# A two-layer decode step on one core: four loads merged into larger ones

## The chip, the cores and the metric

The kernel runs on one core of a Trainium2 chip. The metric is device time in microseconds; the runs of the kernel before agree within 0.1%. Engines are named as the profile names them: PE (matrix multiply), DVE (vector), ACT (activation), POOL (GpSimd), SP (the queue that issues the loads) and 16 DMA engines that carry them.

## The reference

One token (a vector of 512 numbers) goes through two layers with the same weights and the same caches. Each layer is an attention block over a cache of 4096 keys and values in 32 heads of 128, and a dense block with gelu, each behind a layer norm and with a residual. All is float32.

```python
def _A_ref(x, k_cache, v_cache, wq, wo):          # 32 heads, Sk = 4096, Dh = 128
    q = (x @ wq).reshape(B, Sq, H, Dh).transpose(0, 2, 1, 3)
    scores = einsum("bhqd,bhkd->bhqk", q, k_cache) * (Dh ** -0.5)
    p = softmax(scores, axis=-1)
    o = einsum("bhqk,bhkd->bhqd", p, v_cache)
    return o.transpose(0, 2, 1, 3).reshape(B, Sq, H * Dh) @ wo
def _B_ref(x, w1, b1, w2, b2):                    # 512 -> 1376 -> 512
    return einsum("bsf,fd->bsd", gelu(einsum("bsd,df->bsf", x, w1) + b1), w2) + b2
x = x + _A_ref(layernorm(x), k, v, wq, wo)
x = x + _B_ref(layernorm(x), w1, b1, w2, b2)
x = x + _A_ref(layernorm(x), k, v, wq, wo)
x = x + _B_ref(layernorm(x), w1, b1, w2, b2)
```

The keys and values of a layer are 134 MB and don't fit on the core, so almost all of them are read twice.

## The kernel before, in words

The 32 heads are taken in `G = 8` groups of four (`J = 4`). A group's K, and its V, is 8 MB: `C = 8` chunks of 1 MB, each of four quarters (one head each, `U = 512` columns); `NC = 4 * U` is one chunk's width. All large data lie in one tile, `arena`. It holds a ring of three places of 8 MB (`A_AT`, `C_AT`, `B_AT`) for K and V in turn; behind them stand `SHARED`, `SCRATCH`, `TURNED`, `PAIR` (weights of the queries and of the output for one group) and `KEPT_K`.

All loads are issued by SP through one helper (L108), in the order of the program, and SP waits in that order: a load that must wait for its place to come free holds every later one. A load is a DMA of 128 rows.

For a group, `scores` multiplies each chunk of K (8 matmuls in the trace per chunk) into the PSUM tile `pS`, `exponentials` and `weights` make the softmax weights (DVE, ACT, PE in a chain; the last copy is L247), and `values` multiplies each chunk of V into `pO`, again 8 matmuls per chunk. For most groups only two chunks of V go through PE (`partly`) and DVE does the rest. The helper `blocks(src, g, home, pieces)` loads a block in the given pieces and yields its chunks; PE can begin a chunk when its piece has landed. Without `pieces` the block comes as one load. `head` (DVE L286 to L294) turns `pO` into the heads' outputs.

Layer one goes through the groups 0 to 7. Its last group (`final`) loads K as two halves (`HALVES`) and V in the pieces of `LAST` (4, 2, 1 and 1 chunks), and runs all of V on PE. Behind it come `wo`, W1 in four loads and, in `mlp`, W2 in five loads, each issued when PE has read the part of W1 that lay there; `behind_w2` issues the next loads while PE runs through W2. The fourth load of W1 overlaps `SCRATCH` and so waits on SP for DVE L290.

Layer two begins with the groups 7 and 6: V of both, K of group 7 and some of K of group 6 are still on the core. What is missing of K of group 6 is fetched by `begin_k(home, n)`, `n` quarters (of 0.25 MB) at a time. Two such loads of four quarters go to `C_AT`, the place of the K that PE is reading in the scores of group 7, chunk by chunk; each is issued behind the chunk that it overwrites. Then the groups 5 to 0 follow, the last with `HALVES` and `LAST` again, and then `wo`, W1 and W2, here all in places of their own.

`idle` is a matmul by zeros that keeps PE busy between pieces of V; its result is not used.

Of the kernel before, what the change touches and what calls it, by code (L numbers as in the profile page):

```python
# [23 lines left out]
C = 8  # L24
# [5 lines left out]
NC = 4 * U  # L30
# [7 lines left out]
A_AT, B_AT, C_AT = RING  # L38
# [7 lines left out]
HALVES = ((0, 4), (4, 8))  # L46
# [4 lines left out]
FRONT = 192  # L51
CELLS = 239
W1_AT_END = ((0, 2), (2, 3), (3, 4))
LAST = ((0, 4), (4, 6), (6, 7), (7, 8))
W2_AT_CHANGE = ((0, 2), (2, 5), (5, 8), (8, 10), (10, 11))
W2_AT_END = ((0, 4), (4, 8), (8, 10), (10, 11))

# [2 lines left out]
def decode_layers(ctx: ExitStack, tc: tile.TileContext, vectors, k, v, w, w1, w2, out):  # L60
# [42 lines left out]
    def at(first, n):  # L103
        return arena[:, first : first + n]

    def load(first, src):
        t = at(first, src.shape[-1])
        tc.keep_in_program_order(nc.sync.dma_start(t, src))  # L108
        return t
# [4 lines left out]
    def quarters(first):  # L114
        return [at(first + U * j, U) for j in range(4)]

    def part(src, g, a, b):
        return src[g][:, NC * a : NC * b]

    def of_w(row, i, n):  # L120
        return w[row][:, NC * i : NC * (i + n)]
# [33 lines left out]
    def of_32(t, n, i=0):  # L155
        return t[:, : 32 * n].rearrange("p (c q) -> p c q", q=32)[:, :, i]
# [4 lines left out]
    def pairs(t):  # L161
        return t[:, :8].rearrange("p (c i) -> p c i", i=2)
# [61 lines left out]
    def scores(z, c, kt):  # L224
        for j in range(J):
            matmul(pS[32 * j : 32 * j + C, :], z[:, C * j + C - 1 - c : C * j + 2 * C - 1 - c], kt[j],
                   start=(c == 0), stop=(c == C - 1))

    def exponentials(sc, nsc, between=None):
        nc.vector.tensor_reduce(ml[:, 0:1], pS, axis=AX.X, op=ALU.max)  # L230
        m, bias = small("m"), mt
        nc.vector.transpose(mt, ml)
        nc.vector.tensor_reduce(m, mt[:, :C], axis=AX.X, op=ALU.max)
        nc.vector.tensor_scalar(mb[:, :C], m.to_broadcast([P, C]), nsc, None, op0=ALU.mult)  # L234
        nc.vector.transpose(bias, mb)  # L235
        if between:
            between()
        p = at(SCRATCH, U)
        nc.scalar.activation(p, pS, AF.Exp, bias=bias[:, 0:1], scale=sc, accum_out=ml[:, 0:1])  # L239
        return p  # L240
# [39 lines left out]
    def sum_up(t):  # L280
        for j in range(J):
            matmul(pO[32 * j : 32 * j + 4, :], one.to_broadcast([P, 4]), t[j], start=False, stop=True)

    def head(rl, last=False):
        ot = at(SCRATCH, U)
        nc.vector.transpose(ot, pO)  # L286
        o, on = small("o", 4), on_wide
        own = at(SCRATCH, 4 * 129).rearrange("p (b q) -> p b q", q=129)[:, :, :P]
        own = own.rearrange("p b (d q) -> p d b q", q=32)[:, :, :, 0]
        nc.vector.tensor_reduce(o, own, axis=AX.X, op=ALU.add)  # L290
        if last:
            nc.vector.tensor_scalar(on[:, :4], o, rl, None, op0=ALU.mult)  # L292
        else:
            nc.vector.tensor_scalar(in_quarters(on, 4), o.unsqueeze(1).to_broadcast([P, J, 4]), rl, None,  # L294
                                    op0=ALU.mult)
        return on
# [7 lines left out]
    def out_product(on, wt, to, narrow=False):  # L304
        for d in range(4):
            if narrow:
                for j in range(J):
                    matmul(to[32 * j : 32 * j + 1, :P], on[:, d : d + 1], wt[:, d, P * j : P * (j + 1)],
                           start=(d == 0), stop=(d == 3))
            else:  # L310
                matmul(to, on[:, d : d + P], wt[:, d, :], start=(d == 0), stop=(d == 3))
# [47 lines left out]
    def blocks(src, g, home, pieces=((0, C),)):  # L359
        for a, b in pieces:  # L360
            load(home + NC * a, part(src, g, a, b))
            for c in range(a, b):
                yield c, quarters(home + NC * c)
# [29 lines left out]
    def add_up(acc, own):  # L393
        t = small("acc", 4)
        nc.vector.scalar_tensor_tensor(t, own, 1.0, acc, op0=ALU.mult, op1=ALU.add)
        return t


    def group(z, acc, ahead, k_blocks, out_behind=C - 2):
        for c, t in k_blocks:  # L400
            scores(z, c, t)
            if ahead and c == SUM_BEHIND:
                t, rl, wt = ahead
                sum_up(t)
                on = head(rl)
            if ahead and c == out_behind:
                out_product(on, wt, pO)
        p = exponentials(sc, nsc)
        if ahead:
            acc = add_up(acc, of_32(turned(pO, wide=True), 4))  # L410
        return acc, *weights(p)
# [8 lines left out]
    negm, z, sc, nsc = first_queries(xs, s, wq_t, wide=True)  # L420
    acc = pairs(xs)[:, :, 0]
    ahead = None
    for g in range(G):
        final = g == G - 1
        k_home, v_home = RING[2 * g % 3], RING[(2 * g + 1) % 3]
        acc, pt, rl = group(z, acc, ahead, blocks(k, g, k_home, HALVES if final else ((0, C),)))
        ahead = None
        if g == G - 2:
            nc.scalar.copy(at(KEPT_K, 2 * U), at(k_home + NC * C - 2 * U, 2 * U))
        if g < G - 2:  # L430
            partly(pt, blocks(v, g, v_home), v_home)
            pair = load(PAIR, of_w(g % 2, g, 2))
            z = next_queries(xs, negm, by_four(pair[:, NC:]), to=pS)
            ahead = added(v_home), rl, by_four(pair[:, :NC])
            continue
        for c, t in blocks(v, g, v_home, LAST if final else ((0, C),)):
            values(c, pt, t, c)
            if final and c in (5, 7):
                idle(pS)
            if g == G - 2:  # L440
                for j in range(J):
                    i = 4 * c + j - KEPT_V // U
                    if i >= 0:
                        nc.scalar.copy(pK[i], t[j])
        if final:
            wo_t = by_four(load(PAIR, of_w(g % 2, g, 1)))
            for i in range(3):
                load_w1(SHARED, i, i + 1)
            own = head_out(rl, wo_t, last=True, home=ident)
            load_w1(SHARED, 3, 4)  # L450
        else:
            pair = load(PAIR, of_w(g % 2, g, 2))
            acc = add_up(acc, head_out(rl, by_four(pair[:, :NC])))
            wq_t = by_four(pair[:, NC:])
            z = next_queries(xs, negm, wq_t)
# [5 lines left out]
    def begin_k(home, n):  # L461
        a = len(k_t)
        load(home, k[G - 2][:, U * a : U * (a + n)])
        k_t.extend(at(home + U * i, U) for i in range(n))
# [16 lines left out]
    g = G - 2  # L481
    negm, z, sc, nsc = first_queries(xs, s, wq_t)
    make_identity(nc, ident)
    acc = pairs(xs)[:, :, 0]
    wq_t = by_four(at(SHARED, NC))
    begin_k(PAIR + NC, 4)
    for c in range(C):
        scores(z, c, quarters(C_AT + NC * c))
        if c < 2:
            begin_k(C_AT + NC * c, 4)  # L490
        if c == 5:
            begin_k(C_AT + 2 * NC, 12)
            k_t += [at(KEPT_K, U), at(KEPT_K + U, U)]
# [5 lines left out]
    pt, rl = weights(p)  # L499
# [3 lines left out]
    acc = add_up(acc, of_32(turned(pO), 4))  # L503
# [8 lines left out]
    pt, rl = weights(exponentials(sc, nsc))  # L512
    for c in range(C):
        values(c, pt, v_t[4 * c : 4 * c + 4], c)
    acc = add_up(acc, head_out(rl, by_four(pair[:, NC:])))
    z = next_queries(xs, negm, by_four(pair[:, :NC]))

    turned_at[0] = at(TURNED, P)
    homes, ahead = (A_AT, C_AT, B_AT), None
    for n in range(2, G):  # L520
        g, final = G - 1 - n, n == G - 1
        k_home, v_home = homes[(2 * n - 1) % 3], homes[2 * n % 3]
        acc, pt, rl = group(z, acc, ahead, blocks(k, g, k_home, HALVES if final else ((0, C),)),
                            C - 1 if final else C - 2)
        if not final:
            by_pe = BY_PE_AT_BEGIN if n == 2 else BY_PE
            partly(pt, blocks(v, g, v_home, ((0, 6), (6, 8)) if n == 2 else ((0, C),)), v_home, by_pe)
            pair = load(PAIR, of_w(g % 2, g - 1, 2))
            z = next_queries(xs, negm, by_four(pair[:, :NC]), to=pS)
            ahead = added(v_home, by_pe), rl, by_four(pair[:, NC:])  # L530
            continue
        for c, t in blocks(v, g, v_home, LAST):
            values(c, pt, t, c)
            if c in (5, 7):
                idle(pS)
        wo_t = by_four(load(PAIR, of_w(g % 2, g, 1)))
        for a, b in W1_AT_END:
            load_w1(A_AT, a, b)
        for a, b in W2_AT_END:
            load_w2(A_AT + 11 * U, a, b)  # L540
        own = head_out(rl, wo_t, last=True)
# [46 lines left out]
```

## Time and profile before

| | |
|---|---|
| median of 3 runs | 673.24 us (672.96 to 673.5) |
| profiled execution: span | 670.3 us, 2.9 us under the median of the runs |
| mean granted clock of PE | 0.793 |
| PE, DVE, ACT, POOL busy | 384.4, 372.6, 22.8, 4.8 us |
| load queue | 11088 packets, 285.61 MB, 99.1% of 16 engines' span |

The profiled execution has no time of its own other than its span (first to last instruction); what lies around it is the difference to the median. In the rows below, a line of the timeline has the start, the length, the engine, the line of the program, the operation, what it writes and reads, how many instructions were merged, and in brackets the idle time before it and what ended that. A chain's line has start, length, and what the time went to. Times are in us from the start of the span.

### The profile page before, as it was taken

To read this page: it belongs to the slowest core of one execution; us is meant where nothing else is said; L and a number is where in the kernel's file an instruction comes from. 1 tells how busy PE (TensorE), PEld (TensorE's weight loads), DVE (VectorE), ACT (ScalarE), POOL (GpSimd) and SP (SyncE) were. 2 spreads that over 40 slices of the span, in tenths; PEclk is the share of its full clock that TensorE was granted. 3 is DMA by queue.
4 is the path that set the end of the run, shared out by engine and by line. 5 is a ranking of instruction groups with operands and counts; after the bars stand their busy time and mean duration, and the time that the engine had idled before them with its cause. 6 is when DMAs were issued, how large, how long until landed. Compare 5 with 4: busy or idle time off the path is not lost. (4 is left out here: it accounts for less than half of the span.)

```text
span 670.3 us, 5537 instructions
## 1 busy us (share of the span) xinstructions
PE 384.4 (57%) x2342; PEld 109.2 (16%) x2342; DVE 372.6 (56%) x480; ACT 22.8 (3%) x48; POOL 4.8 (1%) x23
## 2 busy tenths in 40 slices
PE   3533842636618546286768878737617456074586
PEld 1101210101102101021214222111102112011122
DVE  2059388395793965932112221392893966938822
ACT  0010000000000000002000110000000000000000
POOL 1000000000000000000000000000000000000000
PEclk9567785877678658778979998977669868687789
DMA  9999999999999999999999999999999999999996
GB/s 376 438 439 438 434 438 438 405 464 435 438 430 408 430 438 439 438 438 421 426 416 402 431 452 423 437 440 431 426 434 416 457 439 438 435 423 407 438 420 286
DMA packets 11256, 285.97 MB, mean 427 GB/s; under 512 B 1504, under 2 KB 1504, under 8 KB 3296
## 3 DMA queue, kind: packets, MB, share of 16 engines
q1 hardware_dynamic: 11088, 285.61, 99.1%
q8 instruction: 18, 0.29, 0.2%
q14 instruction: 6, 0.05, 0.0%
q10 hardware_dynamic: 144, 0.01, 0.0%
HBM read 285.62 MB, written 0.00 MB: 426 GB/s over the span
## 5 line engine op out<-in xcount | busy, mean ns | idle before, releaser
L264 DVE TENSOR_TENSOR arena<-arena 128x2048 f32<-128x2048 f32 (+4 forms) x44 | 260.7, 5924 | 16.6 <-DMA arena<-in_v 15.9
L112 PE MATMUL pS<-arena,front 128*8 128x512 f32 x1036 | 152.0, 713 | 174.9 <-DMA arena<-in_k 164.5
L112 PE MATMUL pO<-arena 128*4 128x512 f32 x504 | 81.7, 800 | 26.1 <-DMA arena<-in_v 24.5
L112 PE MATMUL pO<-arena,cells 128*128 128x512 f32 (+4 forms) x376 | 82.7, 506 | 17.2 <-POOL cells L186 6.7
L112 PEld LDWEIGHTS pS<-arena,front 128*8 128x8 f32 x1036 | 30.6, 102 | 289.1 <-DVE arena L264 141.9
L286 DVE STREAM_TRANSPOSE arena<-pO 128x512 f32<-128x512 f32 x16 | 11.5, 717 | 110.1 <-PE pO L112 110.1
L112 PE MATMUL pS<-arena,cells 128*1 128x128 f32 (+1 forms) x328 | 55.8, 385 | 18.5 <-DMA arena<-in_w 15.8
L170 DVE STREAM_TRANSPOSE arena<-pO 32x128 f32<-32x128 f32 x64 | 20.0, 312 | 59.0 <-PE pO L112 58.4
L112 PEld LDWEIGHTS pO<-arena,cells 128*128 128x128 f32 (+3 forms) x376 | 28.7, 122 | 64.7 <-issue 35.8
L230 DVE TENSOR_REDUCE cells<-pS 128x1 f32<-128x512 f32 x16 | 11.1, 692 | 50.1 <-PE pS L112 49.8
L244 PE MATMUL pO<-front,arena 128*128 128x128 f32 x64 | 12.0, 318 | 46.2 <-ACT arena L239 46.2
L112 PEld LDWEIGHTS pS<-arena,cells 128*1 128x1 f32 (+1 forms) x328 | 23.9, 120 | 61.2 <-issue 52.8
L239 ACT ACTIVATE arena<-pS,cells 128x512 f32<-128x512 f32 x16 | 12.4, 777 | 507.1 <-DVE cells L235 507.1
L112 PEld LDWEIGHTS pO<-arena 128*4 128x4 f32 x504 | 13.5, 99 | 76.2 <-issue 66.3
L244 PEld LDWEIGHTS pO<-front,arena 128*128 128x128 f32 x64 | 7.6, 154 | 60.2 <-ACT arena L239 59.1
L170 DVE STREAM_TRANSPOSE arena<-pS 32x128 f32<-32x128 f32 x44 | 13.7, 312 | 1.6
L249 DVE STREAM_TRANSPOSE cells<-cells 128x32 f32<-128x32 f32 x16 | 3.4, 214 | 15.9 <-ACT arena L239 15.7
L390 DVE MEMSET pS<- 128x512 f32 x11 | 5.3, 485 | 1.2
L174 DVE STREAM_TRANSPOSE arena<-pS 128x128 f32<-128x128 f32 x3 | 1.0, 317 | 8.9 <-PE pS L112 8.9
L199 DVE TENSOR_SCALAR cells<-cells,pS 128x4 f32<-128x4 f32 x4 | 0.9, 234 | 7.9 <-PE pS L112 7.9
L112 PE MATMUL pO<-arena,front 128*128 128x128 f32 (+2 forms) x18 | 5.1, 382 | 0.0
L247 DVE COPY arena<-pO 128x128 f32<-128x128 f32 x16 | 4.2, 261 | 0.7 <-PE pO L244 0.5
(62 smaller groups left out, 72.5 us busy)
## 6 DMA issues: line engine op xcount, KB each, us to landing
arena<-in_w SPq DMA_DIRECT2D x13, 2048.0 KB, 11.2
arena<-in_k SPq DMA_DIRECT2D x4, 4096.0 KB, 24.9
arena<-in_v SPq DMA_DIRECT2D x2, 4096.0 KB, 38.7
arena<-in_w SPq DMA_DIRECT2D x6, 1024.0 KB, 21.1
arena<-in_v SPq DMA_DIRECT2D x3, 2048.0 KB, 42.5
arena<-in_v SPq DMA_DIRECT2D x1, 6144.0 KB, 30.2
arena<-in_w SPq DMA_DIRECT2D x6, 688.0 KB, 25.9
arena<-in_v SPq DMA_DIRECT2D x4, 1024.0 KB, 46.0
```

The lines of the kernel that those rows point to most:

```text
L112: tc.keep_in_program_order(nc.tensor.matmul(*a, **kw))
L170: turn = nc.vector.transpose(t[q], src[q, P * j : P * (j + 1)])
L174: nc.vector.transpose(t, src[:, :P])
L199: nc.vector.tensor_scalar(xc, pairs(xs)[:, :, 0], nm, None, op0=ALU.add)
L230: nc.vector.tensor_reduce(ml[:, 0:1], pS, axis=AX.X, op=ALU.max)
L239: nc.scalar.activation(p, pS, AF.Exp, bias=bias[:, 0:1], scale=sc, accum_out=ml[:, 0:1])
L244: tc.keep_in_program_order(nc.tensor.transpose(pT[:, b].rearrange("p j r -> p (j r)"), p[:, P * b : P * (b + 1)], ident))
L247: nc.vector.tensor_copy(pt, pT[:, :, :, :C].rearrange("p b j c -> p c j b"))
L249: nc.vector.transpose(lt, ml)
L264: tc.keep_in_program_order(nc.vector.tensor_tensor(*a, **kw))
L286: nc.vector.transpose(ot, pO)
L390: nc.vector.memset(pS, 0.0)
```

## The change

Four loads fewer, with the same bytes to the same places:

1. K of the last group of layer one is one load instead of two halves. (Layer two's last K keeps its halves.)
2. V of the last group of layer one is three loads of five, two and one chunks, instead of four loads of four, two, one and one.
3. The same for V of the last group of layer two, by the same constant `LAST`. In both, one `idle` matmul pair moves from behind chunk 5 to behind chunk 6.
4. At the change of layers, two loads of four quarters of group 6's third piece of K become one of eight. It is issued behind chunk 1 of the scores instead of behind chunks 0 and 1.

```diff
-LAST = ((0, 4), (4, 6), (6, 7), (7, 8))
+LAST = ((0, 5), (5, 7), (7, 8))
...
-        acc, pt, rl = group(z, acc, ahead, blocks(k, g, k_home, HALVES if final else ((0, C),)))
+        acc, pt, rl = group(z, acc, ahead, blocks(k, g, k_home))
...
         for c, t in blocks(v, g, v_home, LAST if final else ((0, C),)):
             values(c, pt, t, c)
-            if final and c in (5, 7):
+            if final and c in (6, 7):
                 idle(pS)
...
         scores(z, c, quarters(C_AT + NC * c))
-        if c < 2:
-            begin_k(C_AT + NC * c, 4)
+        if c == 1:
+            begin_k(C_AT, 8)
         if c == 5:
             begin_k(C_AT + 2 * NC, 12)
...
         for c, t in blocks(v, g, v_home, LAST):
             values(c, pt, t, c)
-            if c in (5, 7):
+            if c in (6, 7):
                 idle(pS)
```

## The prediction, on record before the result

> **What bounds the kernel now.** I read the page first (the slices, the queues, the issues), then the chain that ended last, then the stages that the edits touch, as a timeline. The page says what kind of kernel this is:
>
> ```profile
> span 670.3 us, 5537 instructions
> DMA  9999999999999999999999999999999999999996
> GB/s 376 438 439 438 434 438 438 405 464 435 438 430 408 430 438 439 438 438 421 426 416 402 431 452 423 437 440 431 426 434 416 457 439 438 435 423 407 438 420 286
> q1 hardware_dynamic: 11088, 285.61, 99.1%
> HBM read 285.62 MB, written 0.00 MB: 426 GB/s over the span
> ```
>
> The DMA engines are busy in every slice until the last. Slices that carry only large transfers move 438 GB/s; nothing in the span is faster for long. So this is one stream of 285.6 MB, and PE and DVE matter only where they are late in freeing room for it. The chain agrees:
>
> ```profile
> 601.86 45.74 DMA arena<-in_v
> 647.60 0.02 issue
> 647.61 18.66 DMA arena<-in_w
> 666.27 0.04 issue
> 666.32 0.62 PE pS L112 x16
> ```
>
> From the last issues of V to 666.27 the end is the ring emptying itself; only some 4 us of compute stand behind it. An edit can therefore gain in two ways (less overhead inside the stream, a shorter tail) and lose in one (the ring runs dry because an issue came too late). The sum is made against the profiled execution: span 670.3, and the median 673.24 stands 2.9 above it; I take that margin as unchanged.
>
> **The price of a transfer.** The calls to the loading helper, by source, and its quickest landing:
>
> ```profile
> L108 SPq DMA_DIRECT2D arena<-in_w x33: 327/328/432, 0.7 to 651.2; - x33
> L108 SPq DMA_DIRECT2D arena<-in_k x22: 327/382/453, 1.2 to 600.4; - x22
> L108 SPq DMA_DIRECT2D arena<-in_v x21: 327/328/432, 13.1 to 602.3; - x21
> DMA to landing us min/median/max: 4.9/27.9/55.9
> ```
>
> 76 loads and the store of the result make 77 transfers, and 11088 packets / 77 = 144 per transfer, 9 on each of 16 engines. Upper bound of the price: at 438 GB/s the bytes alone need 652 us; the stream runs from about 2 to 666.3, so 12.3 us are overhead of every kind, 0.16 per transfer. Lower bound: nothing. For the value I use the last V of the first layer, where three pieces follow each other and PE waits for the first and for the last of them:
>
> ```profile
> 322.31 3.70 PE L112 MATMUL pO<-arena,cells 128*128 128x512 f32 x8 [1.58 <-DVE cells L395]
> 327.65 7.05 PE L112 MATMUL pS<-arena,front 128*8 128x512 f32 x64 [1.65 <-DVE front L220]
> 331.03 0.18 PEld L112 LDWEIGHTS pS<-arena,front 128*8 128x8 f32 x8 [0.68 <-DMA arena<-in_k]
> 338.22 0.27 DVE L247 COPY arena<-pO 128x128 f32<-128x128 f32 x1
> 340.82 7.25 PE L112 MATMUL pO<-arena 128*4 128x512 f32 x48 [2.66 <-DMA arena<-in_v]
> 348.00 1.12 PE L112 MATMUL pS<-arena,front 128*128 128x512 f32 x2
> 350.46 1.04 PE L112 MATMUL pO<-arena 128*4 128x512 f32 x8 [0.36 <-DMA arena<-in_v]
> 351.57 0.72 DVE L286 STREAM_TRANSPOSE arena<-pO 128x512 f32<-128x512 f32 x1 [13.01 <-PE pO L112]
> ```
>
> Four chunks of 1.049 MB come in 350.46 - 340.82 = 9.64 us; at 438 GB/s they need 9.58. That leaves 0.02 per boundary. Between 0.02 and 0.16 I take 0.07, nearer to the measured row because it is the very place of the edit: four transfers fewer give 0.28 us (0 to 0.64). The 0.33 to 0.43 us that each issue takes on SP is off the path: the small pieces of V are issued 46 us ahead of their landing (a row under edit 4).
>
> If every transfer paid its start inside the stream, the price would be the quickest landing, 4.9 us, less 2.4 us of data, 2.5 us each. The Trainium skill ("DMA: Bandwidth & Descriptors", Anatomy of one DMA) gives about 2.0 us fixed per DMA, for the path issued from GpSimd, and by that the sum would be -8 us. This trace does not bear it out in a full queue: 0.02 us per boundary above. It is kept as a rival below.
>
> **Each edit.** (1) *The first layer's last K whole.* The issue stays at its place, so nothing changes in the stream but one boundary. On PE it changes much. Now the first half's scores run from 327.65 and the second half's from 331.03. Whole, all 64 matmuls start when the second half is in: 331.03 - 0.07 = 330.96. PE has by then been idle since 326.01, 4.9 us, and starts at a lower clock, as in this window view (columns: window, length, PE, PEld, DVE, ACT, POOL, granted clock, DMA share, GB/s):
>
> ```profile
> 334.49:337.91 3.42, 0.69 (x8) 0.42 (x4) 1.93 (x8) 0.87 (x2) 0.00 (x0) 1.00 1.07 455
> 337.91:341.32 3.41, 0.75 (x6) 0.14 (x8) 0.61 (x4) 0.00 (x0) 0.00 (x0) 0.50 0.81 346
> 341.32:344.74 3.42, 3.42 (x20) 0.59 (x16) 0.00 (x0) 0.00 (x0) 0.00 (x0) 0.50 0.99 422
> ```
>
> After a window with 0.69 us of work the clock is 0.50 until a window has been full. The rows nearest to the new situation, and the extremes:
>
> ```profile
> 380.86 7.05 PE L112 MATMUL pO<-arena 128*4 128x512 f32 x64 [0.41 <-DVE arena L247]
> 401.41 9.39 PE pO L112 x64
> 543.54 7.43 PE pS L112 x40
> 621.85 4.98 PE L112 MATMUL pS<-arena,front 128*8 128x512 f32 x32 [6.70 <-DVE pS L390]
> 646.34 6.39 PE L112 MATMUL pO<-arena 128*4 128x512 f32 x48 [0.39 <-DVE arena L247]
> 653.72 1.90 PE L112 MATMUL pO<-arena 128*4 128x512 f32 x16
> ```
>
> Scores: at best 7.05 (the warm row of 64), at worst 7.43 + 24 x 0.11 = 10.0, nearest 4.98 (32 after 6.70 us of idleness) + 3.5 (32 warm) = 8.5. They end at 338.0, 339.5 or 341.0 instead of 334.7. From there to the weights of V the trace takes 338.49 - 334.70 = 3.8: ready at 341.8, 343.3 or 344.8 instead of 338.5.
>
> (2) *The first layer's last V as five, two, one.* Five chunks are in at 340.82 + 2.4 = 343.2, so the late PE hardly waits for them. Nearest row for values and the filler matmuls: 646.34 to 655.62 in the second layer, 9.28 us, which gives 352.6; at worst 344.8 + 9.39 + 1.06 = 355.3; at best PE again waits for the last chunk, 351.5 as now. The filler that moves from behind chunk 5 to behind chunk 6 is the same 1.1 us; its cover was the wait for chunk 6, and now it is the wait for chunk 7. So the head of this layer is later by **s = 0, 1.1 or 3.8 us**; I take 1.1.
>
> What hangs on that head: a load of W1 on SP, which waits for DVE L290 and holds all later SP issues behind it; then every piece of W2 waits for PE to have read a piece of W1, and the next weights for four steps of W2.
>
> ```profile
> SPq L108 <- DVE cells L290: 21.2, 1, 21.2
> 359.58 0.76 PE L112 MATMUL pO<-arena,cells 128*2 128x344 f32 x8 [0.27 <-DMA arena<-in_w]
> 363.63 0.33 SPq L108 DMA_DIRECT2D arena<-in_w  x1
> arena<-in_w SPq DMA_DIRECT2D x1, 1024.0 KB, 6.4
> DMA  9698998998998899999987799999999999999999
> ```
>
> PE's own slack there is about 0.3 (its wait at 359.58). The load issued at 363.63 took 6.4 us to land; the same size in an empty ring took 4.9, so 1.5 us of backlog cover it. But the last row, the DMA share in 40 slices from 362 to 368, falls to 7 tenths near 365.2: some engines are dry already, and for them the cover is 0. So the ring loses between s - 0.3 - 1.5 and s - 0.3: for s = 1.1 between 0 and 0.8, and I take 0.3, nearer to zero, since the stream ends with its slowest engine and that one had backlog. A gap in a full stream is never made good.
>
> (3) *The second layer's last V as five, two, one.* PE starts these values at 646.34 behind DVE L247, not behind V, and has no wait for V up to 655.62. Five chunks land 2.4 us later than four did, some 642.5. Order of work changes, its sum does not: 0 beyond the boundary.
>
> (4) *Two quarters of K in one.* The first quarter is issued one chunk of scores later (0.86 us).
>
> ```profile
> arena<-in_v SPq DMA_DIRECT2D x4, 1024.0 KB, 46.0
> arena<-in_k SPq DMA_DIRECT2D x4, 1024.0 KB, 7.6
> ```
>
> The quarters of K (second row) land 7.6 us after issue against 4.9 in an empty ring: 2.7 us of cover for 0.86 of delay. The scores that read them stand behind row 380.86, so after 387.9. Price 0; with the cover gone it would be at most 0.86.
>
> **Sum.** -0.28 + 0.3 = 0.0: **673.3 us**. A difference under 0.2%, 1.35 us here, can hardly be told from no change.
>
> **Rivals.**
> *The clock is down in both phases and the ring runs dry.* s = 3.8, loss 2.0 to 3.5, less 0.28: 675.0 to 676.5. For it: the 0.50 windows above, and that row 401.41 paid 2.3 us at just such a place. Against: rows 380.86 and 327.65 ran warm, and a window's place relative to the work decides. It becomes slower by over 0.2% from a loss of 1.63, s above 1.9 to 3.4. The Trainium skill ("TensorE: Matmul & The Clock Gate", Part 1) says that the clock halves after an idle window of about 3.4 us and that the windows run freely; the trace agrees with its first half (the window of 3.41 us above), and if the second holds, executions of the changed kernel should differ among themselves.
> *PE's lateness is absorbed entirely* by the wait for the last chunk and the backlog: 673.24 - 0.28 = 673.0.
> *Each transfer costs its start.* 4 x 2.5 = 10 us, 663.2; against it stand the 0.02 us.
> *Nothing happens:* boundaries are free and the cover holds, 673.2.
>
> **Chances.** Forecast (a partial loss, 672.7 to 674.5) 0.54; both phases cold 0.26, of it 0.21 beyond 674.6; absorbed 0.12; nothing 0.04; transfers dear 0.04. So faster by over 0.2%: 0.04; within: 0.75; slower: 0.21. The range runs from all four at 0.16 (672.6) to the middle of the cold case, 672.5 to 675.5.
>
> **What would show it.** The scores of the last K of the first layer as one run of 64 starting near 331.0 and lasting 8 to 10 us; DVE L286 behind it at 351.5 to 355; the DMA share near 365 deeper than 7 tenths if the ring runs dry; the second layer unchanged but for a common shift; the last W2 landing at 666.3 plus that shift. I am wrong if the stream before 327 shifts, if the second layer's tail lengthens by itself, or if the head is late by 3 us and the end is not.

## The result: slower by half a per cent

| | before | changed |
|---|---|---|
| median of 4 runs each | 673.37 us | 676.32 us (676.15 to 677.19) |
| ratio to before, 95% interval | | 1.0051 [1.0037, 1.0066] |
| profiled execution: span, own time | 670.3, about 672.1 | 674.6, 676.4 |
| transfers on the load queue | 77 | 73 |

The forecast was 673.3, within 0.2%. The time lies 0.8 us above its range, in the rival that was given 0.26. Every execution whose span is listed takes 1.7 to 1.9 us beside it, so the execution profiled before took about 672.1 (670.3 and 1.8), 1.1 us under the median that it was set against. That is why the two spans differ by more (4.3 us) than the medians (2.95 us).

The changed kernel's page has the four transfers gone, with the same bytes:

```profile
span 674.6 us, 5528 instructions
GB/s 389 431 424 436 436 435 435 423 449 436 435 431 415 457 431 429 435 435 425 428 415 308 426 440 428 425 455 432 436 435 408 460 428 431 432 428 426 436 417 274
q1 hardware_dynamic: 10512, 285.61, 98.6%
```

10512 / 144 = 73 transfers. In the row of GB/s (40 slices of the span) one slice stands out: the 22nd, 354 to 371 us, moved 308 GB/s where the kernel before moved 402. That is 94 GB/s over 16.9 us, 1.6 MB or 3.6 us of stream. The other slices are near those of before. The timeline of PE at that place, and what follows it:

```profile
331.00 9.55 PE L112 MATMUL pS<-arena,front 128*8 128x512 f32 x64 [4.19 <-DMA arena<-in_k]
343.29 1.11 PE L244 MATMUL pO<-front,arena 128*128 128x128 f32 x4 [2.74 <-ACT arena L239]
344.79 8.62 PE L112 MATMUL pO<-arena 128*4 128x512 f32 x56 [0.38 <-DVE arena L247]
353.34 1.12 PE L112 MATMUL pS<-arena,front 128*128 128x512 f32 x2
354.40 1.04 PE L112 MATMUL pO<-arena 128*4 128x512 f32 x8
355.51 0.72 DVE L286 STREAM_TRANSPOSE arena<-pO 128x512 f32<-128x512 f32 x1 [10.70 <-PE pO L112]
356.50 0.33 SPq L108 DMA_DIRECT2D arena<-in_w  x1
```

The scores start at 331.00, as forecast, and take 9.55 us where they took 7.05. The seven chunks of V that follow take 8.62. DVE L286 starts at 355.51, 3.94 us later than before, and the load of W1 that waits for it (last row) is issued at 356.50. The next rows are windows of the changed kernel: the last three columns are PE's granted clock, the DMA share and GB/s. The first four rows show the clock in the scores and in the values, the others the DMA engines behind the head:

```profile
329.25:332.67 3.42, 1.67 (x9) 0.33 (x13) 0.00 (x0) 0.00 (x0) 0.00 (x0) 0.50 0.89 383
332.67:336.08 3.41, 3.41 (x21) 0.66 (x17) 0.00 (x0) 0.00 (x0) 0.00 (x0) 0.50 0.89 384
342.91:346.32 3.41, 2.64 (x12) 0.98 (x16) 1.14 (x6) 0.33 (x2) 0.00 (x0) 0.50 0.99 425
346.32:349.73 3.41, 3.41 (x20) 0.60 (x16) 0.00 (x0) 0.00 (x0) 0.00 (x0) 0.50 0.98 413
356.00:357.00 1.00, 0.73 (x14) 0.23 (x16) 0.63 (x3) 0.00 (x0) 0.00 (x0) 1.00 0.50 209
357.00:358.00 1.00, 0.81 (x32) 0.50 (x20) 0.12 (x1) 0.00 (x0) 0.00 (x0) 1.00 0.76 110
360.00:361.00 1.00, 1.00 (x12) 0.47 (x5) 0.11 (x3) 0.00 (x0) 0.00 (x0) 1.00 0.71 115
362.00:363.00 1.00, 1.00 (x12) 0.63 (x12) 0.00 (x0) 0.00 (x0) 0.00 (x0) 1.00 0.60 197
356.00:366.00 10.00, 7.93 (x97) 3.58 (x96) 3.31 (x18) 0.21 (x1) 1.18 (x4) 1.00 0.78 250
```

and the last window of the kernel before:

```profile
356.00:366.00 10.00, 8.26 (x106) 3.93 (x104) 2.04 (x12) 0.21 (x1) 0.55 (x1) 1.00 1.00 395
```

The clock was 0.50 for two windows in the scores and again for two in the values. From 356 to 366 the ring (the loads that are issued and not yet landed) moved 250 GB/s instead of 395, in several holes: the first around the issue of the last load of W1, further ones among the pieces of W2. That is 1.45 MB, 3.3 us at 438 GB/s. The end of the chain is as it was, only later:

```profile
605.83 45.67 DMA arena<-in_v
651.50 0.02 issue
651.52 18.92 DMA arena<-in_w
670.44 0.04 issue
670.49 1.04 PE pS L112 x24
```

The last weights are in at 670.44 instead of 666.27: +4.2 in these two executions, and 3.97 of it is there at the last issue of V (605.83 instead of 601.86). The 10 us just shown give 3.3 of it.

### The profile page after: what moved, and what is told of

Read it like the earlier page. It is cut to its first block, busy times and chain, and to the rows that moved or that the text cites. A ratio compares the mean times of both kernels' runs of the same rounds, so it can differ in the third digit from the quotient of the medians.

```text
span 674.6 us, 5528 instructions
## 1 busy us (share of the span) xinstructions
PE 390.4 (58%) x2342; PEld 111.2 (16%) x2342; DVE 372.5 (55%) x480; ACT 22.8 (3%) x48; POOL 4.8 (1%) x23
## 3 DMA queue, kind: packets, MB, share of 16 engines
q1 hardware_dynamic: 10512, 285.61, 98.6%
## 5 line engine op out<-in xcount | busy, mean ns | idle before, releaser
L112 PE MATMUL pO<-arena,cells 128*128 128x512 f32 (+4 forms) x376 | 84.7, 511 | 18.2 <-POOL cells L186 6.6
L286 DVE STREAM_TRANSPOSE arena<-pO 128x512 f32<-128x512 f32 x16 | 11.5, 716 | 107.4 <-PE pO L112 107.4
L112 PE MATMUL pS<-arena,cells 128*1 128x128 f32 (+1 forms) x328 | 59.0, 394 | 18.6 <-DMA arena<-in_w 15.7
```

What stands on the lines that cost most here:

```text
L112: tc.keep_in_program_order(nc.tensor.matmul(*a, **kw))
```

## The experiments

Theory: PE's late scores and its halved clock make the first layer's head late, and the ring of loads runs dry behind it. Each kernel is measured beside runs of the kernel before on the same chip (medians 672.57, 672.7 and 672.93 in the three groups).

**The whole K alone**

```diff
-        acc, pt, rl = group(z, acc, ahead, blocks(k, g, k_home, HALVES if final else ((0, C),)))
+        acc, pt, rl = group(z, acc, ahead, blocks(k, g, k_home))
```

> The kernel before with one edit alone: the first layer's last K as one load. Theory (PE starts its scores late and at half clock, the head of the first layer is 3.9 us late, and the ring of loads runs dry behind it): all of the loss is here, 676.3 to 676.8 us, the head (DVE L286) near 355.5 and DMA under 350 GB/s from 356 to 366. Rival one (the pieces five, two, one of V make PE late): 673.2, head near 351.6. Rival two (the merged quarters of K leave the ring dry): 673.2.

Measured: 675.11 (672.34 to 676.8 in 10 runs), ratio 1.0029 [1.0014, 1.0044]. The profiled execution had its head at 354.93 and 284 GB/s from 356 to 366; its own time was 676.3. So one edit alone can cost the whole loss, but not in every execution: three of the ten took 672.3 to 672.8. The two rivals are out as sole causes.

**All but the whole K**

> The changed kernel with the first layer's last K as two halves again; the other three merged transfers stay. Theory: 673.0 to 673.2 (three transfers at 0.07 us less than before), head within 0.3 of 351.57, no dry ring. Rival one or two (V's pieces or the merged quarters): it keeps the loss, 676.2 or a share of it above 674.5.

Measured: 675.04 (674.63 to 676.34), ratio 1.0042 [1.0028, 1.0055], head at 353.70. The expectation of 673.1 missed: there is a second cause, and it too makes the head late. Its timeline shows the five-chunk piece of V:

```profile
327.54 7.19 PE L112 MATMUL pS<-arena,front 128*8 128x512 f32 x64 [1.64 <-DVE front L220]
337.46 1.11 PE L244 MATMUL pO<-front,arena 128*128 128x128 f32 x4 [2.74 <-ACT arena L239]
343.27 8.33 PE L112 MATMUL pO<-arena 128*4 128x512 f32 x56 [4.70 <-DMA arena<-in_v]
```

With halves of K the scores are early, PE then waits 4.70 us for five chunks of V, and begins them at half clock (0.50 from 343 to 346): 8.33 us for seven chunks. They are done at 351.60; before, six were done at 348.07 and the seventh at 350.10, since four chunks could begin 2.4 us earlier and the low clock was over sooner.

**The first layer's V alone** (five, two, one there only, with the filler pair behind chunk 6)

> The kernel before with one edit alone: the first layer's last V as five, two, one. Theory: PE waits for the five chunks until 343.3 instead of 340.8, always after more than 3.4 us of idleness, so it always starts them at half clock; head at 353.0 to 353.8, time +1.5 to +2.6, 674.2 to 675.3, and no execution as fast as before. Rival (the loss of the run without the whole K needs its edits together): 672.4 to 672.9.

Measured: 675.31 (674.3 to 676.07 in 9 runs), ratio 1.0033 [1.0024, 1.0043]; head at 353.41. No run was as fast as the kernel before. So the first layer's V costs about 2.4 us by itself, and the whole K up to 4. They don't add up, because both delay the same start of the values: 343.09 here, 344.36 with the whole K alone, 344.79 with both. The clock at that start, here:

```profile
343.00:346.00 3.00, 2.91 (x16) 0.60 (x20) 0.00 (x0) 0.00 (x0) 0.00 (x0) 0.50 0.99 423
```

**The two edits that leave the first layer's attention alone** (one load for two quarters of K; V five, two, one in the second layer only)

> The kernel before with the two edits that leave the first layer alone: the two quarters of K in one, and the second layer's last V as five, two, one. Theory (all of the loss is behind the late head of the first layer): as before, 672.3 to 672.7, head within 0.2 of 351.6. Rival (the merged quarter, or the second layer's tail, carries a share, hidden in the run without the whole K): above 673.5.

Measured: 672.52 against 672.7, ratio 1.0 [0.9991, 1.0009], head at 351.53, 398 GB/s from 356 to 366. They cost nothing, and bring nothing that can be measured.

**A late head by itself** (`n` is 2, then 4, in the kernel before)

```diff
         for c, t in blocks(v, g, v_home, LAST if final else ((0, C),)):
+            if final and c == 7:
+                for _ in range(n):
+                    idle(pS)
             values(c, pt, t, c)
```

> The kernel before with two more pairs of filler matmuls (2.1 us of PE) ahead of the last chunk of V in the first layer; all loads as before. It measures what a late head alone costs. Theory (the ring has next to no cover behind the head, as the changed kernel's 3.9 us late head and 4.3 us longer span say): +1.6 to +2.1, 674.9 to 675.5. My recorded prediction's middle (cover of about 0.8): +1.0 to +1.3. Rival (the loss of the changed kernel comes from elsewhere): 673.2 to 673.5.

> The kernel before with four more pairs of filler matmuls (4.3 us of PE) ahead of the last chunk of V in the first layer, so a head about 3.6 us later; loads as before. Theory (the ring has no cover there: each us of late head is a us of time): +3.6 to +4.2 on the kernel before, 676.2 to 676.8. Rival (a cover of 0.8 to 1.5, as I had it on record): +2.1 to +2.8, 674.7 to 675.4.

Measured: 674.76, ratio 1.0032 [1.0019, 1.0044], with n = 2, and 676.85 (3 runs), ratio 1.0066 [1.0051, 1.0082], with n = 4. The wait for the last chunk absorbed part of the fillers, and the heads were at 353.02 and 355.06, 1.45 and 3.49 later than before. With every load as before, a late head alone gives the changed kernel's time and its dry ring (n = 4):

```profile
356.00:366.00 10.00, 7.75 (x97) 3.58 (x96) 2.91 (x16) 0.21 (x1) 1.19 (x4) 1.00 0.80 253
```

**The changed kernel kept warm, and the whole K kept warm** (fillers in the two waits, so that PE's clock stays up)

```diff
-    def group(z, acc, ahead, k_blocks, out_behind=C - 2):
+    def group(z, acc, ahead, k_blocks, out_behind=C - 2, warm=0, warm_late=0):
         for c, t in k_blocks:
+            if c == 0:
+                for _ in range(warm):
+                    idle(pS, of=B_AT)
             scores(z, c, t)
...
+        for _ in range(warm_late):
+            idle(pO, of=B_AT)
         p = exponentials(sc, nsc)
...
-        acc, pt, rl = group(z, acc, ahead, blocks(k, g, k_home))
+        acc, pt, rl = group(z, acc, ahead, blocks(k, g, k_home), warm=3 if final else 0, warm_late=2 if final else 0)
```

(`final` is the first layer's last group alone. The lines with a minus are those of the changed kernel, and of the kernel before with the whole K.)

> The changed kernel, with filler matmuls (zeros, results unused) on PE in the first layer's last group: three pairs (3.2 us) while it waits for the whole K, two pairs (2.1 us) in the gap before the softmax weights. Theory with the clock as its larger part: the scores take 7.1 us from 331.0, the values run at full clock, the head comes at 351.6 to 352.2 and the time is 673.0 to 673.8. Rival (the late arrival itself, with the clock only a by-product): the head stays later than 353.5 and the time above 675.

> The kernel before with the whole K alone, and the same fillers as in the warm run (three pairs while PE waits for K, two in the softmax gap); V keeps its pieces four, two, one, one. Theory (with V's first piece at its old size it is the clock alone that makes the head late): scores 7.1 us, head 351.6 to 352.2, time 672.5 to 673.2, and the spread of 4.5 us among executions of the whole K alone gone. Rival (the whole K is late by itself, warm or not): head later than 353, time above 674.

Measured, changed kernel with fillers: 674.13 (672.8 to 677.07), ratio 1.0024 [1.0008, 1.004]. The whole K alone with fillers: 672.95 (672.6 to 674.99, 8 of 10 under 673.7; why two took 673.94 and 674.99 is not shown), ratio 1.0008 [0.9999, 1.0018]. The second one's timeline:

```profile
331.10 7.05 PE L112 MATMUL pS<-arena,front 128*8 128x512 f32 x64 [1.42 <-DMA arena<-in_k]
341.96 5.45 PE L112 MATMUL pO<-arena 128*4 128x512 f32 x48 [0.42 <-DVE arena L247]
350.45 1.04 PE L112 MATMUL pO<-arena 128*4 128x512 f32 x8 [1.01 <-DMA arena<-in_v]
351.56 0.72 DVE L286 STREAM_TRANSPOSE arena<-pO 128x512 f32<-128x512 f32 x1 [9.59 <-PE pO L112]
```

Scores in 7.05, six chunks of values in 5.45, and PE waits again for the last chunk: the head is at 351.56, as before the change. So the whole K is harmful by the clock alone; at full clock its later start is hidden. With V's five chunks as well, the fillers bring back only a part: the profiled execution's head was at 353.23, between the two that were expected. PE waits 1.65 us for the five chunks and loses its clock once more (first row below). That execution took 677.07, the longest of its six and more than its head explains. Behind 366 its ring moved 374 GB/s (second row) where the kernel before moved 422; the clock had fallen again there, and two stretches of 24 matmuls on W2 took PE 1.30 and 1.43 us, where such a stretch took 0.84 to 0.86 before.

```profile
342.90:346.30 3.40, 3.05 (x16) 0.67 (x20) 0.00 (x0) 0.00 (x0) 0.00 (x0) 0.59 0.98 419
366.00:380.00 14.00, 12.36 (x148) 5.03 (x152) 1.81 (x13) 0.00 (x0) 0.98 (x4) 0.88 0.99 374
```

Whether the five chunks would do harm at full clock was not run. An estimate says no: six chunks took 5.45 us at full clock, so seven from 343.1 would end near 349.5 and the filler pair near 350.5, when the last chunk lands anyway (350.45).

**The whole K, two single executions**

> The kernel with the whole K alone once more, one look, for its spread of 672.3 to 676.8 among executions. Theory (the place of the clock's windows relative to the work decides): if the time is under 673, the values of V ran at full clock within 1 us of their start and the head is before 352.3; if it is over 675, both scores and values began at half clock and the head is after 354. Rival: the head is equally late in both.

> As the look before it, a second one: the same two readings, by its time.

Measured: 677.09 and 673.31. Head at 355.94 in the first and 352.02 in the second. Two windows of each (clock is the third column from the end), the execution of 677.09 first, then that of 673.31:

```profile
343.00:346.00 3.00, 1.99 (x12) 0.89 (x16) 1.13 (x6) 0.58 (x2) 0.00 (x0) 0.57 0.96 407
346.00:349.00 3.00, 3.00 (x20) 0.54 (x16) 0.00 (x0) 0.00 (x0) 0.00 (x0) 0.50 1.00 423
```

```profile
343.00:346.00 3.00, 2.58 (x27) 0.72 (x29) 0.69 (x5) 0.00 (x0) 0.00 (x0) 1.00 0.98 415
346.00:349.00 3.00, 3.00 (x32) 0.54 (x20) 0.00 (x0) 0.00 (x0) 0.00 (x0) 1.00 1.03 434
```

The same program ran the values at half clock in one execution and at full clock in the other; the heads differ by 3.9 us and the times by 3.8. The scores began at half clock in both and took 9.74 and 8.75 us. The second time lies between the two that were named, and its values and its head are those of the fast case.

**More cover in the ring** (the changed kernel with one load moved)

```diff
+            begin_k(PAIR + NC, 4)
             own = head_out(rl, wo_t, last=True, home=ident)
             load_w1(SHARED, 3, 4)
...
-    begin_k(PAIR + NC, 4)
     for c in range(C):
         scores(z, c, quarters(C_AT + NC * c))
```

> The changed kernel, with one load moved and nothing else: the first 1 MB of group 6's K (its place is free by then) is issued ahead of the fourth load of W1 instead of in the second layer, so it stands in the ring, 2.4 us of data, while the head is late. Theory (the loss is the ring running dry behind the late head): recovers 2 to 2.8 of about 4 us, 673.6 to 674.4, with the head as late as before the move (355 or so). Rival (the time is set by the longer chain on PE through the change of layers, the dry ring only shows it): 676 and more.

This load overwrites weights that the second layer still reads, so the queries of its first group come from other numbers; the amount of work is the same. Measured: 674.64 (674.27 to 677.88 in 5 runs), ratio 1.0043 [1.0027, 1.006]. By medians that is 1.9 above before, where the changed kernel was 3.0; by the ratios, whose intervals overlap, the gain is not certain. Less than expected either way. The profile shows why (rows of this kernel):

```profile
356.00:366.00 10.00, 7.76 (x104) 3.57 (x100) 2.68 (x15) 0.21 (x1) 1.18 (x4) 1.00 0.99 390
373.00:379.00 6.00, 6.00 (x60) 1.54 (x64) 0.21 (x2) 0.00 (x0) 0.35 (x1) 1.00 0.82 302
```

The hole behind the late head (its head was at 354.56) is filled, 390 GB/s. A new one opens at 373 to 379, where the moved load used to be under way: 302 against 427 in the same window of the kernel before, 0.75 MB or 1.7 us. So most of the loss was moved with the load: this execution, 3.0 us late at the head, was still 1.6 above 672.7.

**The price of a transfer** (V of the first layer's groups 0 to 5 in eight loads each, in the kernel before)

```diff
-            partly(pt, blocks(v, g, v_home), v_home)
+            partly(pt, blocks(v, g, v_home, tuple((i, i + 1) for i in range(C))), v_home)
```

> The kernel before, with V of the first layer's groups 0 to 5 loaded in eight loads of one chunk instead of one load each: 42 transfers more, where every place is free and PE and DVE are far from late. It measures the price of a transfer in a full ring. By the 0.07 us on record: +2.9 us, 675.6; by its ends 0.02 and 0.16: +0.8 to +6.7; if a transfer paid its start in the stream (2.5 us): over +60.

Measured: 674.39 against 672.93, +1.46 us for 42 transfers, ratio 1.0021 [1.0011, 1.003]: 0.035 us each (0.018 to 0.048). Four transfers are worth 0.14 us.

## Why the prediction was wrong

Put in one table: how much later DVE L286 starts than 351.57, the rate of the ring from 356 to 366, and the profiled execution's own time less 672.7, the median before in the second group.

| kernel | head later by | GB/s | time above before |
|---|---|---|---|
| two edits elsewhere | 0.0 | 398 | 0.3 |
| whole K, fillers | 0.0 | 395 | -0.1 |
| whole K, second single execution | 0.45 | 387 | 0.6 |
| two fillers | 1.45 | 321 | 1.5 |
| V of layer one | 1.84 | 323 | 1.7 |
| all but K | 2.13 | 342 | 2.3 |
| whole K | 3.36 | 284 | 3.6 |
| changed kernel | 3.94 | 250 | 3.7 |
| whole K, first single execution | 4.37 | 247 | 4.4 |

In these nine executions one us of late head is one us of time, to within 0.4 us. The runs of the kernel before spread from 672.0 to 674.0 themselves, so the table cannot tell whether the first half us costs anything.

Two further executions lie above that line: four fillers (3.49 later, 678.4, the longest of three) and the changed kernel with fillers (1.66 later, 677.07). Both lost more behind 366. With four fillers the ring moved 387 GB/s instead of 422 from 366 to 380, 1.1 us, and at the end of the kernel PE's last 56 matmuls took 3.21 us at a clock of 0.50, where 64 took 1.93 before. Also left out are the moved load and the run with 42 transfers more: there the head is 2.13 later because the whole stream is (the last group's scores start at 330.21 instead of 327.65), the ring is full behind it (393 GB/s), and the time is 1.7 above.

- *The delay s* is the step that failed most, a term that was mis-sized: 1.1 taken, 3.9 measured, just past its worst end of 3.8. The scores took 9.55 against the 8.5 taken and 10.0 at worst; from them to the weights it took 4.2 against 3.8; and from the weights (344.8, the worst end) to the head 10.7 against 9.28. These three make 2.9 us, and the clock was 0.50 in part of each. By the prediction's own rule of cover (between s - 1.8 and s - 0.3), s = 3.9 would have given 675.1 to 676.6; with s = 1.1 and no cover at all the time would have been 674.1. The middle row was taken for each phase as if the clock's state were a size. For the values it was one of two in the runs of the whole K (six chunks in 7.6 to 7.9 us, or in 5.33).
- *The cover behind the head* failed too. The prediction took 1.5 us from a landing of 6.4 against 4.9 in an empty ring, saw the DMA share fall to 7 tenths near 365, and took a loss of 0.3 for a delay of 1.1. Its own other end, next to no cover, was right: two fillers made the head 1.45 later and the time 1.5 longer, with every load as before. The row with the dip was the better witness. The landing time of one load said nothing of the pieces of W2 ahead of it, each of which needs the head too.
- *The top of the range* was put at 675.5 as the middle of the cold case; the middle of 675.0 to 676.5 is 675.75. The result lies above both.
- *"Five chunks are in at 343.2, so the late PE hardly waits for them"*: true beside the late K (PE waited 0.38 us, for DVE), and it hid that this edit is harmful by itself, 1.8 us of delay (V alone).
- *The price of a transfer*, 0.07 taken, 0.035 measured; 0.28 and 0.14 are both too small to see here. The rival of 2.5 us each is out.
- *The second layer's V and the merged quarters* at 0: right, by the run of the two alone.
- *The rival of the cold clock* described what happened: place, mechanism and time (675.0 to 676.5). Its second half, that executions should differ among themselves, is shown for the whole K alone. The rule from the Trainium skill ("TensorE: Matmul & The Clock Gate", Part 1), that the windows run freely, agrees with the two single executions of the whole K; the four runs of the changed kernel, all between 676.15 and 677.19, don't show it. Whether the five chunks of V exclude the good case there or four runs were too few stays open.
- *The margin* between span and time is 1.8; the 2.9 taken also held what the profiled execution lay under the median.

## What to carry to other kernels

In this kernel, bound by one stream of loads, a merged transfer is worth some tens of nanoseconds (0.035 us by the run with 42 more), and its cost was what the consumer lost by waiting for the larger piece. Follow such a wait to the next load that is issued because of it: where the ring was already thin, every us of lateness was lost for good. And a small piece can be worth its transfer just by keeping PE busy enough that its clock stays up, as the two halves of K did here.

## What the runs showed of the hardware

A transfer more in a full ring cost 0.035 us (42 of them, 1.46 us), with rows of 8 KB instead of 64 KB. One program, the whole K alone, took 672.3 to 676.8 us on one chip. In two executions of it on another chip, 673.31 and 677.09 us, the values ran at a clock of 1.00 in the first and at 0.50 for their first 5 us in the second. Filler matmuls, 2.7 us of PE in one wait and 2.0 in the next, removed most of that spread (672.6 to 675.0).
